# Zero fills in 2 MB pairs of 16 KB rows, and the w_o gradient stored with 2 KB rows

## The chip, the cores and the metric

The kernel runs on one core of a Trainium2 chip. The time is what the device reports for one execution, in microseconds (us). The kernel before took 599.43 us (median of three runs, 598.24 to 599.79). A profile of one execution goes with it; its span runs from the first to the last instruction.

In what follows PE is the engine for matrix products, DVE and ACT are the engines for element-wise work, POOL and SP are the engines that issue most of the DMA transfers here. Each core has 16 DMA engines, and all transfers run on them. POOL's transfers stand in the queue that the profile calls q0, SP's in q1.

## The reference

One token passes through a modulated attention block with a cache and a modulated gated feed-forward block, and then all gradients are computed for the output's gradient `grad_out`.

```python
def _A_ref(x, k_cache, v_cache, wq, wo):      # Hq 32, 4 cache groups, Sk 65536, W 4096
    q = (x @ wq) ...
    k = k_cache[:, :, Sk - W:, :] ...         # the last 4096 positions alone
    v = v_cache[:, :, Sk - W:, :] ...
    p = softmax(q k^T * Dh ** -0.5)
    return (p v) @ wo
mod = silu(c) @ w_mod                         # six parts: sa, ca, ga, sb, cb, gb
h = layernorm(x) * (1 + ca) + sa
x = x + ga * _A_ref(h, A_k_cache, A_v_cache, A_wq, A_wo)
h = layernorm(x) * (1 + cb) + sb
x = x + gb * ((sigmoid(h @ w_gate) * (h @ w_up)) @ w_down)
# outputs: x, and the gradients of A_x, k_cache, v_cache, wq, wo, w_gate, w_up, w_down, c, w_mod
```

The gradients of the two caches have the caches' full shape, 4 groups of 65536 rows of 128 numbers each, and all but the last 4096 rows of each group are zero. So most of what the kernel writes is zeros: 2 x 4 regions of 15 MB.

## The kernel before, in words

**Stages.** In order of time (from the profile): loads of the cache windows and of w_q, the query and the scores (to about 67 us); the N stage, 128 steps of products of keys with weighted values (line 640, to about 155 us); the long product stage, in which 64 chunks (`bch`, line 685) of 8 products each combine w_q and w_o (line 695), mixed with the sections of w_mod (to about 306 us); the feed-forward stage, seven blocks of 512 columns of w_gate and w_up and 512 rows of w_down, forward and backward at once (lines 1022 to 1066, to about 480 us); the end stage, which makes and stores the gradients of w_o (`dwo`, line 1139), w_mod (`sec`, `s2`), the caches' last rows (`dV`, `dK`) and w_q (`dwq_tile`).

**Order.** Nothing is reordered by a scheduler: each engine does its instructions in the order in which the program writes them (`tc.manual_schedule()`), and semaphores hold each back until what it reads or overwrites is ready. POOL issues nearly all transfers, in program order, and SP those of w_down, three small rows, some parts of w_mod, and the last stores.

**Zero fills.** The eight zero regions are seen as 128 rows of 120 KB, one row to a partition. They are cut into 120 units of 1 MB, each 128 rows of 8 KB. `zero(n)` (line 153) issues the next n units on POOL from one tile of zeros, which is held in an 8-bit type and widened to 4 bytes by the transfer. Six of the units, at the places NARROW, leave out the first 8 partitions; what they leave is filled by small transfers apart (lines 160 to 167 and 360). The constants Z_* say how many units go at each place of the program. In the N stage and in the product stage the fills are paced: `zero(Z_N[s], recent(mm, 6))` (line 643) makes the fill wait for a product some steps back, and likewise in `bch` (line 697). Z_SM (line 526) is the number of fills that go as soon as the softmax sum's reciprocal is there, just before the N stage. In the feed-forward stage they go at four places of each block (Z_FFN).

**Loads that the fills stand beside.** w_o is loaded in eight parts of 512 rows (`load_wo`, line 337), w_mod in sections (`b_sec`, line 739; `wm_sec`, line 340). Section 2 has the parts of `ga`; `mod_tiles` (line 344) multiplies its eight tiles into ga_ps, sections 4 and 3 likewise into cb_ps and md_ps, and section 5 into g_ps, from which the feed-forward stage's first operands come. `load_ug` (866) and `store_ug` (870) move the up and gate blocks on POOL, `load_wd` and `store_wd` (854, 857) the w_down blocks on SP.

**The gradient of w_o.** A part u of it is the outer product of the attention output's 512 numbers with a row of 1024, made by DVE in the arena's tile `wo_t[u]` as four pieces of 128 partitions. It is stored so that a partition holds four neighbouring rows of the output, 8 KB in one piece:

```python
def dwo_dram(u):
    return out_5[u * 512:(u + 1) * 512, :].rearrange("(p a) n -> p a n", a=4)
```

For that the 512 numbers have to lie in another order than elsewhere. 16 small products (line 1073) and a copy make `o_perm` from `o_col` between the feed-forward stage and the end stage.

**Tiles.** Most data live in one arena of 192 KB per partition; `vt` (line 104) gives the small tiles beside it.

Of the kernel before, what the change touches and what calls it, by code (L numbers as in the profile page):

```python
# [10 lines left out]
P = 128  # L11
FP32 = mybir.dt.float32
BF16 = mybir.dt.bfloat16
# [11 lines left out]
HQ = 32  # L25
# [26 lines left out]
Z_SM = 4  # L52
Z_N = spread(31, 128)
# [5 lines left out]
def kernel(  # L59
# [43 lines left out]

    def vt(shape, name, dt=FP32):
        return pool.tile(shape, dt, name=name)
# [5 lines left out]
    zeros = vt([P, ZW // 2], "zeros", FP8)  # L111
    rows24 = vt([24, P], "rows24", BF16)
# [7 lines left out]
    ones_f = vt([P, P], "ones_f")  # L120
# [3 lines left out]
    for og in (out_2, out_3):  # L124
        for g in range(G):
            region = og[0, g, 0:SKW, :].rearrange("r d -> (r d)").rearrange("(p x) -> p x", p=P)
            for i in range(region.shape[1] // ZW):
                zregions.append(region[:, i * ZW:(i + 1) * ZW])

    narrow = zregions[0:len(NARROW)]
    wide = zregions[len(NARROW):]
    zleft = []
    while narrow or wide:
        if narrow and (len(zleft) in NARROW or not wide):
            zleft.append((narrow.pop(0), True))
        else:
            zleft.append((wide.pop(0), False))
    nlen = len(NARROW)
    ncount = list(range(1, nlen + 1))  # L140
# [12 lines left out]
    def zero(n, after=None):  # L153
        for _ in range(n):
            if len(zleft) <= keep[0]:
                return
            region, narrow_ = zleft.pop(0)
            first = None
            if narrow_:
                nc.gpsimd.inc_swdge_sem([], [], mode="reset_dge_cursor")  # L160
                n = nlen - ncount.pop()
                first = nc.gpsimd.dma_start(
                    out=rest[0:NS, 0:nlen * 128].rearrange("p (t x) -> p t x", t=2)[:, :, n * 64:(n + 1) * 64],
                    in_=zeros[0:NS, 0:64].rearrange("p (t x) -> p t x", t=1).broadcast_to([NS, 2, 64]))
                ins = nc.gpsimd.dma_start(
                    out=region[8:P, :].bitcast(FP32).rearrange("(t p) x -> p t x", t=2),
                    in_=zeros[0:60, :].rearrange("p (t x) -> p t x", t=1).broadcast_to([60, 2, ZW // 2]))
            else:
                ins = nc.gpsimd.dma_start(out=region.bitcast(FP32), in_=zeros[:, :])  # L169
            if after is not None:  # L170
                dep(first or ins, after)

# [80 lines left out]
    def total_bcast(part, ncol, name, scale):  # L253
        ps = new_acc("tot_" + name)
        nc.tensor.matmul(ps[:, 0:ncol], lhsT=ones_f[:, :], rhs=part[:, 0:ncol], start=True, stop=True)
        tot = vt([P, ncol], name)
        ts(tot, ps[:, 0:ncol], float(scale), ALU.mult)
        return tot

    def layernorm_col(x_col, name, gap=lambda: None):  # L260
# [7 lines left out]
        sq = vt([P, KD], name + "_sq")  # L268
# [13 lines left out]
    def layernorm_bwd_col(dln, ln, rstd, name):  # L282
        part = vt([P, 2], name + "_parts")
        nc.vector.reduce_sum(out=part[:, 0:1], in_=dln, axis=AX.X)
        tmp = vt([P, KD], name + "_tmp")
        ttr(tmp, dln, ln, part[:, 1:2])
        means = total_bcast(part, 2, name + "_means", -1.0 / D)
        dx = vt([P, KD], name + "_dx")
        nc.vector.scalar_tensor_tensor(out=dx, in0=ln, scalar=means[:, 1:2], in1=dln, op0=ALU.mult, op1=ALU.add)
        ts(dx, dx, means[:, 0:1], ALU.add, rstd[:, 0:1], ALU.mult)  # L290
        return dx, means
# [41 lines left out]

    def dwo_dram(u):
        return out_5[u * 512:(u + 1) * 512, :].rearrange("(p a) n -> p a n", a=4)
# [293 lines left out]
    for g in range(G):  # L629
        nbank = bank_pair("n_ps", g)  # L630
        for t_ in range(KT):
# [11 lines left out]
            zero(Z_N[s], recent(mm, 6))  # L643
# [41 lines left out]
    def bch(n=1):  # L685
        for _ in range(n):
# [10 lines left out]
            zero(Z_B[nbq - 1 - len(bq)], recent(mm, 3))  # L697
# [228 lines left out]
    assert not bq  # L926
    fold_half(7, 1)
    zero(Z_FOLD[0])
# [90 lines left out]
    zero(Z_FOLD[2])  # L1019
    load_wd(1, 0)  # L1020
    load_wd(1, 1)
    for q in range(NB):
        z = Z_FFN[q]
        more = q + 1 < NB
        for j in range(KD):
# [12 lines left out]
            if j == 3:  # L1038
                store_ug(q, 0, 4)
                zero(z[0])  # L1040
        store_ug(q, 4, 4)
        zero(z[1])
        if more:
# [13 lines left out]
            zero(z[2])  # L1057
# [3 lines left out]
            zero(z[3])  # L1061
# [3 lines left out]
        else:  # L1065
            zero(z[2] + z[3])
# [3 lines left out]
    op_ps = new_acc("op_ps")  # L1070
    for hh in range(4):
        for a in range(4):
            nc.tensor.matmul(op_ps[32 * hh:32 * hh + 32, 8 * a:8 * a + 8], lhsT=ident_f[:, a::4], rhs=o_col[:, hh::4],
                             start=True, stop=True, tile_position=(0, 32 * hh))
    o_perm = kb_col
    cp(o_perm, op_ps[:, 0:HQ])
# [62 lines left out]
    def dwo(u):  # L1139
        for a in range(4):  # L1140
            outer_dve(wo_t[u][:, a, :], o_perm[:, 8 * a + u:8 * a + u + 1], dattn_b)
        nc.gpsimd.dma_start(out=dwo_dram(u), in_=wo_t[u])
# [134 lines left out]
    x2 = vt([P, KD], "x2")  # L1277
# [4 lines left out]
    dcsum = vt([P, KD], "dcsum")  # L1282
# [3 lines left out]
    t1 = vt([P, KD], "dc_t1")  # L1286
# [4 lines left out]
    dct = vt([P, KD], "dct")  # L1291
    addv(dct, dcs01[:, :, 0], dcsum)
    addv(dct, dct, dcs)
    dcv = vt([P, KD], "dcv")
# [8 lines left out]
    dwq_tile(5)  # L1303
    tail = nc.sync
    s2(2, tail)
# [8 lines left out]
    assert not zleft and not narrow and not jobs and not bq  # L1314
# [29 lines left out]
```

## Time and profile before

| | us |
|---|---|
| median of three runs | 599.43 |
| the profiled execution | 599.43 |
| its span | 597.6 |

| engine | busy us | share of the span |
|---|---|---|
| PE | 410.6 | 69% |
| DVE | 337.4 | 56% |
| ACT | 264.5 | 44% |
| POOL | 155.0 | 26% |

| transfers | count, KB each | us from issue to landing (median) |
|---|---|---|
| zero fills, POOL | 114 x 1024 | 16.7 |
| zero fills, narrow, POOL | 6 x 960 | 12.7 |
| stores of 1 MB, POOL (w_o gradient among them) | 28 x 1024 | 19.2 |
| w_o loads, POOL | 8 x 1024 | 12.6 |
| w_mod loads, POOL | 7 x 1024 | 18.9 |
| w_down loads, SP | 14 x 512 | 10.2 |

How to read the profile: its first rows cut the span into 40 slices of 14.9 us, and a digit is the busy share of a slice in tenths. Below them stand the bytes per second of each slice and the packets of each DMA queue; a packet is what one of the 16 DMA engines moves at a time, and a row of a transfer that is up to 8 KB long is one packet, while rows of 1 or 2 KB go in packets of 4 KB. Lines of a timeline give start, duration, engine, source line and operation; in brackets is the idle time of the engine before, and what ended it. Landings are told by the semaphores that the 16 DMA engines raise.

### The profile page before, as it was taken

What the parts mean: (1) busy time and instruction counts of PE and PEld (TensorE: products, weight loads), DVE (VectorE), ACT (ScalarE), POOL (GpSimd) and SP (SyncE); (2) the same over time, 40 slices, a digit from 0 to 9 for tenths busy, and PEclk for the clock granted to TensorE, in tenths of its full rate; (3) what the DMA queues carried; (4) which work ended last, traced back from release to release, by engine and by line L of the source; (5) the groups of instructions that cost most, each with busy time, mean ns of one, the idle gap of its engine ahead of it and who ended that gap; (6) DMA issues with size and microseconds to landing.
All of it is one profiled execution on the core that took longest, in us unless ns stands there. A gap on an engine that the chain in (4) does not pass through costs nothing. (4 is left out here: it accounts for less than half of the span.)

```text
span 597.6 us, 11102 instructions
## 1 busy us (share of the span) xinstructions
PE 410.6 (69%) x4619; PEld 278.0 (47%) x4644; DVE 337.4 (56%) x642; ACT 264.5 (44%) x408; POOL 155.0 (26%) x254
## 2 busy tenths in 40 slices
PE   3997689999999989899974444544444295785210
PEld 3996434334344446556554433434434265585110
DVE  3654599999511020160019495796786886878350
ACT  3479515558211023212225472754744835793110
POOL 3113213212222222222221342323423252131100
PEclk9999799999999999999985555555555586855555
DMA  8999999999999999999999999999999999999996
GB/s 352 418 418 422 412 425 417 429 424 424 428 421 426 422 428 423 422 424 424 421 401 411 419 404 403 398 390 416 401 399 420 419 422 422 422 423 425 426 423 284
DMA packets 44002, 246.63 MB, mean 413 GB/s; under 512 B 5085, under 2 KB 5085, under 8 KB 22496
## 3 DMA queue, kind: packets, MB, share of 16 engines
q0 software_dynamic: 36656, 218.64, 95.3%
q1 hardware_dynamic: 7248, 27.27, 11.9%
q8 instruction: 36, 0.59, 0.4%
q14 instruction: 14, 0.11, 0.0%
q10 hardware_dynamic: 48, 0.01, 0.0%
HBM read 60.30 MB, written 185.60 MB: 411 GB/s over the span
## 5 line engine op out<-in xcount | busy, mean ns | idle before, releaser
L695 PE MATMUL b_ps<-arena 128*128 128x512 bf16 x494 | 113.4, 379 | 1.0 <-issue 0.2
L169 POOL DMA_DIRECT2D out_dram<-zeros x114 | 62.4, 548 | 173.7 <-DMA out_dram<-zeros 47.4
L840 PE MATMUL tp_side<-ident_bf,arena 128*128 128x128 bf16 x432 | 51.7, 300 | 54.7 <-ACT arena L841 46.0
L193 DVE TENSOR_TENSOR arena<-arena 128x2048 bf16<-128x2048 bf16 x64 | 76.5, 1223 | 2.3 <-PE n_ps L640 0.3
L695 PEld LDWEIGHTS <-arena 128*128 128x128 bf16 x512 | 48.7, 98 | 55.9 <-issue 2.9
L840 PEld LDWEIGHTS <-arena 128*128 128x128 bf16 x432 | 44.3, 141 | 62.3 <-issue 62.1
L841 ACT COPY arena<-tp_side 128x1024 bf16<-128x1024 bf16 x54 | 54.0, 1013 | 40.9 <-PE tp_side L840 40.0
L640 PE MATMUL n_ps<-arena 128*128 128x512 bf16 x249 | 65.1, 378 | 6.9 <-DVE arena L193 5.0
L210 DVE CUSTOM_DVE_ANT_0 arena<-arena,scr 128x1024 bf16<-128x1024 bf16 x56 | 66.2, 1220 | 3.5 <-ACT scr L996 3.5
L210 DVE CUSTOM_DVE_ANT_0 junk<-arena,b1k 128x1024 bf16<-128x1024 bf16 x28 | 34.3, 1223 | 32.8 <-DMA arena<-in_B_w_down_dram 32.2
L640 PEld LDWEIGHTS <-arena 128*128 128x128 bf16 x256 | 24.6, 97 | 41.6 <-issue 16.2
L241 ACT ACTIVATE arena<-scr,h 128x1024 bf16<-128x1024 bf16 x35 | 39.3, 1148 | 0.0
L202 DVE CAST arena<-b_ps 128x512 bf16<-128x512 f32 x6 | 4.2, 692 | 61.6 <-PE b_ps L695 61.6
L1173 ACT ACTIVATE arena<-ps_kv 128x512 bf16<-128x512 f32 x48 | 26.1, 680 | 27.5 <-PE ps_kv L1169 27.4
L1169 PE MATMUL ps_kv<-junk,arena 8*128 8x128 bf16 x256 | 27.4, 305 | 13.7 <-DVE arena L206 12.7
L604 ACT CAST arena<-t_ps 128x512 bf16<-128x512 f32 x56 | 30.1, 589 | 12.1 <-PE t_ps L602 12.1
L872 POOL DMA_DIRECT2D out_dram<-arena x28 | 21.3, 765 | 50.2 <-ACT arena L241 43.5
L1169 PEld LDWEIGHTS <-arena 8*128 8x128 bf16 x256 | 25.2, 141 | 15.6 <-issue 15.5
L996 ACT COPY scr<-tp_dug 128x1024 bf16<-128x1024 bf16 x7 | 7.1, 1012 | 41.5 <-issue 41.5
L459 ACT COPY arena<-tp_wq 128x1024 bf16<-128x1024 bf16 x23 | 21.7, 1041 | 8.1 <-PE tp_wq L457 8.1
L868 POOL DMA_DIRECT2D arena<-in_B_w_up_dram x14 | 10.6, 755 | 49.5 <-DMA out_dram<-arena 29.6
L206 DVE TENSOR_SCALAR arena<-arena,cs_col 128x4096 bf16<-128x4096 bf16 (+1 forms) x16 | 16.1, 1024 | 10.4 <-DMA out_dram<-arena 10.3
(305 smaller groups left out, 640.1 us busy)
## 6 DMA issues: line engine op xcount, KB each, us to landing
out_dram<-zeros POOLq DMA_DIRECT2D x114, 1024.0 KB, 16.7
out_dram<-arena POOLq DMA_DIRECT2D x28, 1024.0 KB, 19.2
out_dram<-arena POOLq DMA_DIRECT2D x30, 512.0 KB, 11.4
out_dram<-arena SPq DMA_DIRECT2D x20, 512.0 KB, 8.6
arena<-in_A_wq_dram POOLq DMA_DIRECT2D x8, 1024.0 KB, 20.8
arena<-in_A_wo_dram POOLq DMA_DIRECT2D x8, 1024.0 KB, 12.6
arena<-in_w_mod_dram POOLq DMA_DIRECT2D x7, 1024.0 KB, 18.9
arena<-in_B_w_down_dram SPq DMA_DIRECT2D x14, 512.0 KB, 10.2
```

What stands on the lines that cost most here:

```text
L169: ins = nc.gpsimd.dma_start(out=region.bitcast(FP32), in_=zeros[:, :])
L193: return nc.vector.tensor_tensor(out=out, in0=a, in1=b, op=op)
L210: return nc.vector.tensor_tensor_reduce(out=out, in0=w, in1=b, scale=1.0, scalar=0.0, op0=ALU.mult, op1=ALU.add, accum_out=acc)
L241: return nc.scalar.activation(out=out, in_=b, func=ACT.Copy, scale=col)
L459: nc.scalar.copy(out=blk, in_=tp[:, :])
L604: nc.scalar.copy(out=o, in_=ps)
L640: mm = nc.tensor.matmul(nbank[k][:, :], lhsT=k_nat[:, g, t_ * DH:(t_ + 1) * DH], rhs=vp[:, t_ % 2, 4 * k:4 * k + 4, :].rearrange("p h d -> ...
L695: mm = nc.tensor.matmul(bbank[p][k][:, :], lhsT=a4[:, p, h, :], rhs=wo_t[u][:, a, k * 512:(k + 1) * 512], start=(i == 0 and a == 0), stop= ...
L840: nc.tensor.transpose(tp[:, i * P:(i + 1) * P], blk[:, i * P:(i + 1) * P], ident_bf[:, :])
L841: nc.scalar.copy(out=blk if dst is None else dst, in_=tp[:, :])
L1169: nc.tensor.matmul(ps[:, t4 * DH:(t4 + 1) * DH], lhsT=rows[32 * g:32 * g + HG, t_ * P:(t_ + 1) * P], rhs=hd[32 * g:32 * g + HG, :], start= ...
L1173: nc.scalar.activation(out=o, in_=ps[:, :], func=ACT.Copy, scale=float(scale))
```

## The change

- `zregions` keeps whole regions. They are cut into pairs (128 rows of 16 KB, 2 MB) and singles (8 KB rows); `zero` takes a pair where two units in a row are due and neither is narrow, unless it is called with `paired=False`, as in the feed-forward stage. 40 of POOL's fills are then pairs, 34 singles, 6 narrow.
- `paced` replaces `zero` in the N stage and the product stage: it keeps account of the units owed and issues an even number at the first that is owed, so every second unit goes earlier than its place.
- Z_SM is 6 instead of 4, and Z_N has 29 units instead of 31.
- The gradient of w_o is stored as it is loaded, each partition holding rows 128 apart, in pieces of 2 KB; `o_perm` and what makes it are gone.
- `dwq_tile(5)` is issued by SP instead of POOL.
- The tile of zeros is twice as long. To make room, small tiles share one tile (`tiny`), `ones_f` is one column, `rows24` lies in the arena, and some late vectors lie in tiles that are free by then.

```diff
-Z_SM = 4
-Z_N = spread(31, 128)
+Z_SM = 6
+Z_N = spread(29, 128)
...
     def vt(shape, name, dt=FP32):
+        words = shape[1] if dt == FP32 else (shape[1] + 1) // 2
+        if dt in (FP32, BF16) and words < 8:
+            k = tiny_n[0]
+            tiny_n[0] += words
+            assert tiny_n[0] <= TINY
+            t = tiny_t[:, k:k + words]
+            return t if dt == FP32 else t.bitcast(BF16)
         return pool.tile(shape, dt, name=name)
...
-    zeros = vt([P, ZW // 2], "zeros", FP8)
-    rows24 = vt([24, P], "rows24", BF16)
+    zeros = vt([P, ZW], "zeros", FP8)
+    rows24 = ar(144, 0.25)[0:24, :]
...
-    ones_f = vt([P, P], "ones_f")
+    ones_f = vt([P, 1], "ones_f")
...
+    for k, region in enumerate(zregions):
+        i = nlen if k == 0 else 0
+        n = region.shape[1] // ZW
+        if (n - i) % 2:
+            singles.append(region[:, i * ZW:(i + 1) * ZW])
+            i += 1
+        pairs.extend(region[:, c * ZW:(c + 2) * ZW] for c in range(i, n, 2))
...
-    def zero(n, after=None):
+    def zero(n, after=None, paired=True):
+        while n > 0 and len(zleft) > keep[0]:
...
+            elif paired and n > 0 and pairs and len(zleft) > keep[0] and not zleft[0]:
+                n -= 1
+                zleft.pop(0)
+                ins = nc.gpsimd.dma_start(out=pairs.pop(0).bitcast(FP32), in_=zeros[:, :])
             else:
-                ins = nc.gpsimd.dma_start(out=region.bitcast(FP32), in_=zeros[:, :])
+                if not singles:
+                    pr = pairs.pop()
+                    singles.extend((pr[:, 0:ZW], pr[:, ZW:2 * ZW]))
+                ins = nc.gpsimd.dma_start(out=singles.pop(0).bitcast(FP32), in_=zeros[:, 0:ZW // 2])
...
+    def paced(n, after):
+        owed[0] += n
+        if owed[0] > 0:
+            k = owed[0] + owed[0] % 2
+            owed[0] -= k
+            zero(k, after)
...
-            zero(Z_N[s], recent(mm, 6))
+            paced(Z_N[s], recent(mm, 6))
...
-            zero(Z_B[nbq - 1 - len(bq)], recent(mm, 3))
+            paced(Z_B[nbq - 1 - len(bq)], recent(mm, 3))
...
-    zero(Z_FOLD[0])
+    zero(Z_FOLD[0] - ahead)
...
-                zero(z[0])
+                zero(z[0], None, False)
...
-    op_ps = new_acc("op_ps")
-    for hh in range(4):
-        for a in range(4):
-            nc.tensor.matmul(op_ps[32 * hh:32 * hh + 32, 8 * a:8 * a + 8], lhsT=ident_f[:, a::4], rhs=o_col[:, hh::4],
-                             start=True, stop=True, tile_position=(0, 32 * hh))
-    o_perm = kb_col
-    cp(o_perm, op_ps[:, 0:HQ])
...
     def dwo(u):
         for a in range(4):
-            outer_dve(wo_t[u][:, a, :], o_perm[:, 8 * a + u:8 * a + u + 1], dattn_b)
-        nc.gpsimd.dma_start(out=dwo_dram(u), in_=wo_t[u])
+            outer_dve(wo_t[u][:, a, :], o_col[:, 4 * u + a:4 * u + a + 1], dattn_b)
+        nc.gpsimd.dma_start(out=wo_dram(out_5, u), in_=wo_t[u])
...
-    dwq_tile(5)
     tail = nc.sync
+    dwq_tile(5, tail)
```

## The prediction

> **What bounds the kernel now.** I read the slices first, then the DMA queues, then the waits and timelines of POOL and PE, and last the packet and landing times that the trace keeps for each transfer.
>
> ```profile
> PE   3997689999999989899974444544444295785210
> DMA  8999999999999999999999999999999999999996
> GB/s 352 418 418 422 412 425 417 429 424 424 428 421 426 422 428 423 422 424 424 421 401 411 419 404 403 398 390 416 401 399 420 419 422 422 422 423 425 426 423 284
> DMA packets 44002, 246.63 MB, mean 413 GB/s; under 512 B 5085, under 2 KB 5085, under 8 KB 22496
> q0 software_dynamic: 36656, 218.64, 95.3%
> q1 hardware_dynamic: 7248, 27.27, 11.9%
> ```
>
> No engine but DMA is full from end to end: bytes over rate is the span. What can move the end is the price of the bytes, or an interval in which the queues have nothing. The waits of POOL, which issues nearly everything, say how the queue is fed:
>
> ```profile
> POOL out_dram L169 <- DMA out_dram<-zeros: 47.4, 26, 3.9
> POOL out_dram L169 <- PE n_ps L640: 42.4, 21, 4.0
> POOL out_dram L169 <- PE b_ps L695: 32.6, 13, 5.3
> ```
>
> The first line is POOL waiting for an older transfer. Its issue times and the landings show why: the k-th POOL transfer always waits for the (k-8)-th, so eight are in flight at most, and from 137 to 315 us there are seven at nearly every issue (they land 14 to 23 us after their issue). POOL's timeline in the long product stage shows one issue per landing:
>
> ```profile
> 192.04 0.77 POOL L341 DMA_DIRECT2D arena<-in_w_mod_dram  x1 [1.44 <-DMA out_dram<-zeros]
> 194.19 0.53 POOL L169 DMA_DIRECT2D out_dram<-zeros  x1 [1.37 <-DMA out_dram<-zeros]
> 196.62 0.53 POOL L169 DMA_DIRECT2D out_dram<-zeros  x1 [1.90 <-DMA out_dram<-zeros]
> ```
>
> PE is nearly full there too, so it has to be asked where PE and DMA meet. PE's timeline has two places:
>
> ```profile
> 210.10 2.04 PE L347 MATMUL ga_ps<-cs_bf,arena 128*128 128x1 bf16 x64
> ...
> 250.45 1.74 PE L347 MATMUL cb_ps<-cs_bf,arena 128*128 128x1 bf16 x64
> ...
> 305.55 0.61 PE L789 MATMUL BT_ps<-ident_bf,scr 128*128 128x128 bf16 x8
> 307.92 1.35 PE L347 MATMUL g_ps<-cs_bf,arena 128*128 128x1 bf16 x48 [1.75 <-DMA arena<-in_w_mod_dram]
> ```
>
> The reader is to see that ga_ps takes 0.30 us more than the equal cb_ps: its second half needs the load issued at 192.04, whose last engine landed at 211.14, about when PE gets there. And before the feed-forward stage PE waits 1.75 us for a load.
>
> **Part 1, the fills (zero, paced).** Of 120 MB-units, 80 go as 40 pairs, 34 stay single (27 of them from the feed-forward stage's first fills on), 6 stay narrow. The pair's packet size is nowhere on POOL's queue; I build its price. On one engine the commonest packet of 2 KB takes 84 ns, of 4 KB 159 ns, of 8 KB 309 ns: 9 ns each plus 36.6 ns per KB. The 64 KB that one engine has of a 1 MB fill are 2400 ns by the slope alone. Landing to landing, a fill after a fill takes 2448 ns (mean over the 16 engines, median of 83). So 48 ns per fill belong to packets and to the completion, and a pair, with as many packets and one completion for twice the bytes, can save at most 48: 40 x 48 = 1.9 us. The slow engines lose more: within one fill's landing the first-to-last spread grows from 1.95 us (52.58 to 54.53) to 3.48 us (254.35 to 257.83). They need about (3.48-1.95)/86 = 18 ns more per transfer. If half or all of that is paid per packet, pairs save up to 40 x 66 = 2.6 us. The low bound is nothing saved, and below it a loss, if 16 KB rows are cut: that is a rival below. I take 1.9, since the rows that make it are this same operation, and 2.6 as one end.
>
> POOL's issues fall by 40 x 0.55 us (L169's mean); they run inside the 173.7 us in which POOL waits before them, so they count nothing.
>
> **Part 2, order and pacing.** Each fill's place in q0 decides when the loads behind it land. Counting MB-units in both orders ahead of each load: w_o part 0 has 2 more, part 4 has 3 more, parts 5 to 7, the second w_mod load (b_sec(2,4), 192.04), both of section 4 and the first of section 3 one more; the others, the feed-forward loads too, are equal. One more is 2.45 us later. Only b_sec(2,4) has no slack: with 23 pairs ahead of it (1.1 us saved) it lands 1.35 us later, about 212.5, and PE, at its tiles near 211.1, stalls about 1.4 us. The others have 4.8 us (245.61 against 250.45) or more. Six fills instead of four after rsum: at that issue (67.63) two transfers are still in flight until 71.83, so q0 is covered before and after; nothing.
>
> With pairs, eight in flight are up to 16 MB, so POOL runs with PE and not with the landings. In one queue that changes no order, so I cost it at nothing; the cover is q0's backlog.
>
> **Part 3, SP's loads behind fat packets.** The loads of w_down and two of w_mod on q1 (SP, issued 284.07 to 300.28) were first served at 295.45, 11.4 us after their issue, and from 295.5 to 299.5 had 157 GB/s beside q0's 249. If rows of 16 KB halve q1's turns and double its wait, q1 starts when q0's fills before the feed-forward loads are through: those would take 300.5 us, less 1.9, so about 299 to 301 with PE's 1.4. Then 1 MB at half of the 400 GB/s that 4 KB packets move (5.2 us) and 0.5 MB of 2 KB packets at about 125 (its rate at 304 to 306; 4.2 us) end near 310.4 instead of 308.25. So g_ps and the feed-forward stage start 1 to 3 us later. Does that reach the end? At that stage's last stores (472.72) q0's backlog runs to 478.57, 5.85 us. Fills that are done 1.9 us sooner leave 3.95. A start 2 us later stays under it: nothing.
>
> [...]
>
> **Part 4, w_o's gradient (dwo).** Eight stores of 1 MB go from 8 KB rows to 2 KB rows. Store after store with 8 KB rows: 2453 ns. With 1 KB rows (w_up/w_gate gradients, beside no other queue): 1276 for half, 2552 per MB. Loads with 2 KB rows (w_o after w_o): 2625. Those show as 4 KB packets. Packets alone (2 x 159 against 309) give 9 x 1024 / 16 = 0.6 us in all, the low bound: no shorter row was cheaper in any stage. The ends by rows are 8 x 0.10 = 0.8 and 8 x 0.17 = 1.4; I take 1.1, between the same direction and the same row length. POOL's issue grows from 0.53 to 0.77 us, under 7 in flight.
>
> [...]
>
> The permutation goes: 32 matmuls on PE at 466.6 to 468.1, in PE's slack, and a copy of 0.18 us on the chain at 476.08. DMA has 2 us or more of backlog there: nothing, at most -0.2.
>
> **Part 5, tail and small edits.** dwq_tile(5) goes from POOL to SP. [...] Behind it q0 and q1 still hold work to 591, so the same bytes end at the same time; 0, bounds +-0.5. The packed small tiles, one column of ones, and the memset of zeros (twice as long, under 4.75 us of POOL's wait for vecs): 0.
>
> **Sum.** The profiled execution is 599.43 (span 597.6 and 1.8 around it), also the median of the three. -1.9 + 1.1 = -0.8: **598.6 us**.
>
> **Rivals.** (1) Slow engines gain too. For: their spread collapses in the feed-forward stage (389.09 to 390.94, one at 392.31), so the others wait for them. -2.6 + 0.6 - 0.2, and up to half of that 3.5 us spread: 595.5 to 597.2. (2) The feed-forward stage starts late past its backlog. Place: g_ps; it decides from 3.95 us of delay, and is slower than before from 4.75. If q1's first turn comes 5.5 us late, with PE's 1.4 that is 6.9, and 598.6 + 2.95 = 601.5. Against it: q0's packets turn to 4 KB at about 300 anyway. (3) The row of 16 KB is cut into 4 KB packets, the change does not do what it says: 16 x 159 + 9 = 2553 against 2448 is +0.105 per MB, 80 MB are +8.4, with dwo 608.9. Against: 8 KB rows were not cut, and the instruction queue shows 16 KB packets (at 1010 ns median, 62 ns per KB, dearer than 36.6; that queue feeds no output, so it sets no price here).
>
> **How the numbers follow.** The forecast (597.8 to 600.5) has 0.45, rival 1 0.30, rival 2 0.15, rival 3 0.07, others 0.03. About 0.3% (1.8 us) is what a measurement of this kernel can tell from no change. Faster by that takes rival 1 and little else: 0.31. Within: the forecast and a third of rival 2: 0.47. Slower: 0.22. The range leaves out rival 3 and the ends of 1 and 2: 596.2 to 601.6.
>
> **What would show it.** On the page: about 5100 packets fewer on q0 from fills, 1024 more from dwo. Landing intervals of pairs of 4.85 us or less (right), 4.90 (nothing saved), 5.1 (cut). ga_ps longer by about 1.4 us; g_ps starting after 308.5. dwo's landings 2.55 to 2.63 us apart. The slices of the product stage at 426 to 432 GB/s. What would make it wrong: slices below 9 at 300 to 480 us, or a tail whose last engine is later by more than a microsecond.

## The result, and the profile after

The changed kernel takes 605.01 us (median of 20 executions, 600.81 to 607.84); the kernel before takes 599.41 us (20 executions beside it). The ratio is 1.0079, with a 95% interval of 1.0055 to 1.0103: the change costs 0.8%. I had forecast 598.6 us, and 0.22 for slower. Here and below a ratio leaves out executions more than 1.5% above their kernel's fastest (three of e1's twelve, six of e4's, two of e12's, one of e13's), which the medians keep, so a median can show a larger loss than its ratio. The executions of the changed kernel spread with PE's clock: the nine with the longest times, 606.62 us and above, have a mean granted clock of 0.767 or less, the eleven others, 605.55 and below, 0.768 or more. Which of the two makes the other is not told by this: PE's clock is 0.50 in the feed-forward stage (from 309.98 to 484.06 us in the profile of before, from 316.28 to 490.36 in that of the changed kernel), so a stage that lasts longer lowers the mean too. The profiled one took 607.84 (span 606.1), so its rows show the loss at its largest: 8.4 us more than the profile of before.

The page of the changed kernel, the rows that answer to those shown of before:

```profile
PE   3998679999999989999874454444445196684220
PEclk9998899999999979989995555555555576955555
DMA  8999999999999999999999599999999999999997
GB/s 352 418 418 425 413 429 426 431 428 424 430 426 421 431 429 419 435 419 428 408 412 360 197 404 418 381 397 411 404 405 407 416 420 416 421 419 426 425 423 304
DMA packets 39266, 246.63 MB, mean 407 GB/s; under 512 B 4445, under 2 KB 4445, under 8 KB 23904
q0 software_dynamic: 31776, 217.59, 91.2%
q1 hardware_dynamic: 7392, 28.32, 12.4%
```

PEclk is the clock that PE was granted, in tenths of full speed. The same row of before:

```profile
PEclk9999799999999999999985555555555586855555
```

The reader sees three things. The fills did become cheaper: of the 4th to the 19th slice, eleven are at 425 GB/s or more, where before had five. Nearly all the loss is in one place, the 22nd and 23rd slice (318 to 349 us), with 360 and 197 GB/s. And PEclk has two slices below 9 in the product stage, the 15th and the 18th, where before has 9 until the slice in which that stage ends (the 21st).

Six microseconds at a time, the hole looks like this (stretch; busy time of PE, PEld, DVE, ACT, POOL; granted clock, DMA share, GB/s):

```profile
328.00:334.00 6.00, 2.58 (x46) 2.37 (x47) 5.15 (x14) 1.16 (x3) 0.00 (x0) 0.50 0.79 292
334.00:340.00 6.00, 2.48 (x21) 2.00 (x19) 6.00 (x12) 4.40 (x5) 0.00 (x0) 0.50 0.81 272
340.00:346.00 6.00, 3.03 (x24) 2.54 (x24) 5.86 (x12) 5.85 (x7) 1.94 (x3) 0.50 0.15 55
```

POOL has issued the last fill ahead of the stage by 317.8, and its next instruction is the first store of the feed-forward stage. POOL's timeline, after and then before:

```profile
316.19 1.64 POOL L185 DMA_DIRECT2D out_dram<-zeros  x3
344.06 1.52 POOL L896 DMA_DIRECT2D out_dram<-arena  x2 [26.23 <-ACT arena L266]
```

```profile
320.70 0.53 POOL L169 DMA_DIRECT2D out_dram<-zeros  x1 [1.85 <-DMA out_dram<-zeros]
331.05 1.52 POOL L872 DMA_DIRECT2D out_dram<-arena  x2 [9.82 <-ACT arena L241]
```

Before, three of POOL's transfers were still in flight at that store, and the last fill landed at 339.37, 8.3 us after it. After, the store comes 13.0 us later, the last fill has landed at 334.13, and POOL's queue is empty for 9.9 us.

Why is the stage late? PE's waits between 60 and 330 us, and its timeline at g_ps, the stage's first input:

```profile
PE g_ps L371 <- DMA arena<-in_w_mod_dram: 6.2, 2, 4.4
...
PE md_ps L371 <- issue: 2.2, 1, 2.2
...
PE b_ps L719 <- DMA arena<-in_A_wo_dram: 0.9, 1, 0.9
...
PE ga_ps L371 <- DMA arena<-in_w_mod_dram: 0.8, 1, 0.8
```

```profile
313.98 0.94 PE L371 MATMUL g_ps<-tiny,arena 128*128 128x1 bf16 x32
316.64 0.37 PE L371 MATMUL g_ps<-tiny,arena 128*128 128x1 bf16 x8 [1.71 <-DMA arena<-in_w_mod_dram]
321.46 0.38 PE L371 MATMUL g_ps<-tiny,arena 128*128 128x1 bf16 x8 [4.45 <-DMA arena<-in_w_mod_dram]
```

PE is done with the product stage at 314.15 instead of 306.16, 8.0 us late. Then it waits for the two w_mod tiles that SP loads, wm_sec(5,4) and wm_sec(5,5). SP can issue those only when PE is done with what lies in their place (line 945 of the changed kernel), so they are late with PE. SP's waits between 280 and 325 us say so:

```profile
SPq L365 <- PE b_ps L719: 13.3, 2, 7.4
```

The load wm_sec(5,5) is issued at 308.27 instead of 300.28. It also takes longer, 13.1 us instead of 8.0, and lands at 321.41 instead of 308.25: 13.2 us late, of which 8.0 are PE's and 5.2 its own.

PE's 8.0 us are waits of 0.92 (w_o), 0.77 (ga_ps) and 2.16 us (md_ps), and time at half clock. PE's timeline behind ga_ps, a microsecond of the same stretch, and the same seven products in before:

```profile
210.96 0.94 PE L371 MATMUL ga_ps<-tiny,arena 128*128 128x1 bf16 x32
212.67 0.95 PE L371 MATMUL ga_ps<-tiny,arena 128*128 128x1 bf16 x32 [0.77 <-DMA arena<-in_w_mod_dram]
213.70 3.01 PE L719 MATMUL b_ps<-arena 128*128 128x512 bf16 x7
```

```profile
214.00:215.00 1.00, 1.00 (x4) 0.40 (x3) 0.36 (x3) 0.00 (x0) 0.00 (x0) 0.50 0.94 377
```

```profile
212.21 1.67 PE L695 MATMUL b_ps<-arena 128*128 128x512 bf16 x7
```

Seven products that took 1.67 us in before take 3.01, at a granted clock of 0.50. There are three such stretches between 160 and 310 us, at 213.9, 224.1 and 258.25, each 3.41 us long; before has none. At a clock of 0.50 each can cost PE at most half of its length, 1.7 us.

So the story of this one profile has four links: a load lands later; PE waits and then runs at half clock for a while; SP's last load is issued late and lands later still; POOL's queue runs dry before the stage has anything to store. The experiments take the links one by one.

### The profile page after: what moved, and what is told of

It reads as the page before. It is cut to its first block, busy times and chain, and to the rows that moved or that the text cites. A ratio compares the mean times of both kernels' runs of the same rounds, so it can differ in the third digit from the quotient of the medians.

```text
span 606.1 us, 10967 instructions
## 1 busy us (share of the span) xinstructions
PE 414.2 (68%) x4587; PEld 279.2 (46%) x4612; DVE 338.7 (56%) x641; ACT 264.8 (44%) x408; POOL 138.0 (23%) x213
## 5 line engine op out<-in xcount | busy, mean ns | idle before, releaser
L719 PE MATMUL b_ps<-arena 128*128 128x512 bf16 x494 | 117.8, 389 | 2.1 <-DMA arena<-in_A_wo_dram 0.9
L719 PEld LDWEIGHTS <-arena 128*128 128x128 bf16 x512 | 50.0, 100 | 59.8 <-issue 9.4
L864 PEld LDWEIGHTS <-arena 128*128 128x128 bf16 x432 | 44.8, 142 | 62.3 <-issue 62.1
L180 POOL DMA_DIRECT2D out_dram<-zeros x40 | 21.7, 543 | 134.3 <-PE b_ps L719 52.8
L664 PEld LDWEIGHTS <-arena 128*128 128x128 bf16 x256 | 24.6, 97 | 41.6 <-issue 16.2
L185 POOL DMA_DIRECT2D out_dram<-zeros x34 | 19.3, 570 | 32.1 <-PE q_ps L499 14.3
## 6 DMA issues: line engine op xcount, KB each, us to landing
out_dram<-zeros POOLq DMA_DIRECT2D x34, 1024.0 KB, 13.2
out_dram<-arena POOLq DMA_DIRECT2D x30, 512.0 KB, 10.9
```

The costliest lines, as they stand in the source:

```text
L180: ins = nc.gpsimd.dma_start(out=pairs.pop(0).bitcast(FP32), in_=zeros[:, :])
L664: mm = nc.tensor.matmul(nbank[k][:, :], lhsT=k_nat[:, g, t_ * DH:(t_ + 1) * DH], rhs=vp[:, t_ % 2, 4 * k:4 * k + 4, :].rearrange("p h d -> ...
L719: mm = nc.tensor.matmul(bbank[p][k][:, :], lhsT=a4[:, p, h, :], rhs=wo_t[u][:, a, k * 512:(k + 1) * 512], start=(i == 0 and a == 0), stop= ...
L864: nc.tensor.transpose(tp[:, i * P:(i + 1) * P], blk[:, i * P:(i + 1) * P], ident_bf[:, :])
```

## The experiments

I started with two theories. **Theory A**: the rows of 16 KB, or the 16 MB that pairs put in flight, hold up SP's loads and PE's instruction fetches. **Theory B**: the order is to blame; `paced` issues each pair when its first unit is owed, so one more MB stands ahead of some loads.

This table has the profiled execution of every run; the median and the ratio to the kernel before follow below, run by run. "Load" is the last load that g_ps needs, wm_sec(5,5); "in flight" counts POOL's transfers at the stage's first store; the rate is that of 310 to 345 us. One execution need not be like the median: e3's is the slowest of its twelve, those of e1, e4, e9, e11 and e16 are the fastest or second fastest of theirs.

| kernel | load issued, landed | first store | in flight | GB/s | profiled us |
|---|---|---|---|---|---|
| before | 300.28, 308.25 | 331.05 | 3 | 416 | 599.43 |
| after | 308.27, 321.41 | 344.06 | 0 | 309 | 607.84 |
| e1 8 KB halves | 303.75, 313.33 | 335.91 | 1 | 389 | 602.26 |
| e2 lagging pairs | 301.93, 309.49 | 331.46 | 3 | 414 | 599.04 |
| e3 2 KB rows alone | 304.71, 316.37 | 339.01 | 0 | 376 | 601.97 |
| e4 late fills single | 303.50, 315.03 | 337.67 | 0 | 366 | 603.38 |
| e5 one fill ahead | 311.35, 322.61 | 345.25 | 0 | 330 | 608.45 |
| e6 one pair held | 300.90, 312.20 | 334.85 | 1 | 380 | 602.11 |
| e7 idle products | 307.11, 321.42 | 344.07 | 0 | 315 | 606.81 |
| e8 lag, work in waits | 298.72, 308.81 | 331.43 | 3 | 415 | 598.93 |
| e9 own tile | at 5.85 | 333.00 | 2 | 408 | 599.03 |
| e10 busy 2.4 us | 305.93, 317.41 | 340.06 | 0 | 371 | 603.78 |
| e11 busy 4.8 us | 306.54, 319.58 | 342.23 | 0 | 346 | 604.86 |
| e12 lag, Z_SM 8 | 302.35, 317.03 | 339.68 | 0 | 352 | 603.91 |
| e13 one ahead, busy | 306.03, 317.63 | 340.27 | 0 | 360 | 604.86 |
| e14 lag, own tile | at 5.9 | 333.81 | 2 | 413 | 599.72 |
| e15 e14 and work | at 5.9 | 331.37 | 3 | 416 | 599.75 |
| e16 e14, 2 MB pairs | at 5.8 | 330.96 | 3 | 416 | 597.08 |

Wherever the load is issued by PE's pace, the first store follows its landing by 22.0 to 22.8 us. That is the last two links in one row: when the load is late the store is late, and where at most one transfer is in flight by then, the rate is 389 GB/s or less and the time 601.97 us or more; with two or three it is 408 or more. e3's row shows that the loss can come without any change of the order: its median is 599.31, and this execution, with PE waiting 0.71 us at ga_ps and the load landing at 316.37, took 601.97. The kernel before has executions as slow (up to 603.39), none of them profiled. With the change they are the rule: its fastest of 20 took 600.81. With 35 us at 309 instead of 416 GB/s, after loses 9.0 us there.

### Rows or order: e1, e2, e4

e1 keeps the changed order and drops the rows of 16 KB:

```diff
-                ins = nc.gpsimd.dma_start(out=pairs.pop(0).bitcast(FP32), in_=zeros[:, :])
+                pr = pairs.pop(0)
+                first = nc.gpsimd.dma_start(out=pr[:, 0:ZW].bitcast(FP32), in_=zeros[:, 0:ZW // 2])
+                ins = nc.gpsimd.dma_start(out=pr[:, ZW:2 * ZW].bitcast(FP32), in_=zeros[:, 0:ZW // 2])
```

> The changed kernel with every pair issued as two transfers of 1 MB and 8 KB rows, at the same place, in the same order, with the same wait. Theory A (the rows of 16 KB themselves, or the 16 MB they put in flight, keep SP's loads and PE's instruction fetches waiting, and so the feed-forward stage starts 13 us late): the loss goes; the last SP load before g_ps lands near 308 to 311, POOL's queue stays full at 330 to 345, and the time is that of the kernel before plus 0.5 (w_o gradient): 599.5 to 600.5. Theory B (the order: one MB more ahead of the loads, PE waits at w_o and ga_ps, and the half-clock stretches follow): nothing or little is won, 604 to 606, and ga_ps still waits.

Measured: 607.18 us, ratio 1.0074 (1.0039 to 1.0108). Theory A falls as the cause of the loss: without a single row of 16 KB the loss is about the same (1.0079 for the changed kernel). The sign that I had named for theory B is not in the profile, though: this execution took 602.26, PE came to ga_ps at 212.47, later than in the changed kernel (210.96), and did not wait there.

e2 keeps the pairs and changes when they go:

```diff
-        if owed[0] > 0:
-            k = owed[0] + owed[0] % 2
+        if owed[0] > 1:
+            k = owed[0] - owed[0] % 2
```

> The changed kernel with paced() issuing a pair when two units are owed instead of when the first is, so that no load has more ahead of it than in the kernel before from the product stage on. Theory A: the waits of PE on w_o and ga_ps go, but the loads of SP are as slow as in the changed kernel (about 13 us for wm_sec(5,5)) and PE's wait in md_ps stays: 602 to 605. Theory B: 598 to 599.5, since the pairs' 1.7 us are then won.

Measured: 599.22 us, ratio 1.0002 (0.9980 to 1.0025). This is what theory B said: 40 pairs of 16 KB rows, and the loss is gone (one of the twelve executions still took 605.90). PE's timeline of e2 at ga_ps and g_ps shows no wait at the first and a short one at the second:

```profile
212.06 1.74 PE L371 MATMUL ga_ps<-tiny,arena 128*128 128x1 bf16 x64
...
309.53 0.35 PE L371 MATMUL g_ps<-tiny,arena 128*128 128x1 bf16 x8 [0.74 <-DMA arena<-in_w_mod_dram]
```

The gain that theory B promised as well is hardly there (0.33 us below the median of before, within the interval). In e2's profile the queue is short of work at 94 to 98 us (317 and 346 GB/s) and the feed-forward stage has some slices lower than before's (the 26th 379 against 398).

e4 makes the last seven pairs before the stage single again:

```diff
-            paced(Z_B[nbq - 1 - len(bq)], recent(mm, 3))
+            paced(Z_B[nbq - 1 - len(bq)], recent(mm, 3), nbq - 1 - len(bq) < 40)
...
-    zero(Z_FOLD[0] - ahead)
+    zero(Z_FOLD[0] - ahead, None, False)
```

(the third argument of `paced` goes to `zero` as `paired`).

> The changed kernel with the last seven pairs before the feed-forward stage (from about 265 us on) as singles, so that SP's loads and ug loads stand beside 8 KB rows; 33 pairs stay. Theory A in the form that SP's loads alone matter: wm_sec(5,5) takes 8 us again instead of 13, PE's earlier waits stay, the stage starts 6 to 8 us late instead of 13, and the time falls to 601 to 602.5. Theory B: PE's early waits are what counts, 604 to 605.

Measured: 607.41 us, ratio 1.0069 (1.0035 to 1.0103). SP's last load takes 11.5 us beside rows of 8 KB too, against 13.1 in the changed kernel. Rows of 16 KB beside SP's loads at the end are not needed for the loss.

### One fill: e5, e6

e5 is the kernel before with one number of its pacing moved by one chunk:

```diff
-Z_B = [n + (i in (31, 38)) for i, n in enumerate(spread(29, 43))] + ...
+Z_B = [n + (i in (31, 38)) + (i == 15) - (i == 16) for i, n in enumerate(spread(29, 43))] + ...
```

> The kernel before with one thing changed: one zero fill of 1 MB, paced by the chunk after it, goes on POOL ahead of the second w_mod load of section 2 (b_sec(2,4)) instead of behind it. Theory B (order: ga_ps waits for that load, PE stalls and runs at half clock for some microseconds after, the loads that SP issues behind PE come late, POOL's queue runs dry at 330 to 345): the whole loss from this one fill, 602 to 607, ga_ps with a wait of 1 to 2.5 us. Theory D (it takes several loads one MB later, the w_o parts above all): 599.5 to 600.5.

Measured: 608.05 us, ratio 1.0109 (1.0063 to 1.0155). One fill of 1 MB on the other side of one load costs 8.8 us at the median, 6.5 by the ratio; no pair, no other change is needed. (Two of the six executions took 601.25 and 602.61, the others 607.82 and more.) PE's timeline of e5:

```profile
210.13 0.94 PE L347 MATMUL ga_ps<-cs_bf,arena 128*128 128x1 bf16 x32
213.42 0.97 PE L347 MATMUL ga_ps<-cs_bf,arena 128*128 128x1 bf16 x32 [2.35 <-DMA arena<-in_w_mod_dram]
...
317.07 1.14 PE L347 MATMUL g_ps<-cs_bf,arena 128*128 128x1 bf16 x40
322.66 0.37 PE L347 MATMUL g_ps<-cs_bf,arena 128*128 128x1 bf16 x8 [4.45 <-DMA arena<-in_w_mod_dram]
```

With a wait of 2.35 us at ga_ps PE is 10.9 us late at g_ps (317.07; in before it was ready at 306.16).

e6 is the opposite: the changed kernel with the one pair behind that load.

```diff
-        if owed[0] > 0:
+        if owed[0] > 0 and not hold:
...
-            paced(Z_B[nbq - 1 - len(bq)], recent(mm, 3))
+            paced(Z_B[nbq - 1 - len(bq)], recent(mm, 3), nbq - 1 - len(bq) in (14, 15))
```

(`hold` is a new third argument of `paced`.)

> The changed kernel with one pair moved: the one that paced() issues at chunk 14, ahead of b_sec(2,4), is held until that load has been issued. All else, the w_o parts with one MB more ahead of them too, is as in the changed kernel. Theory B: 598.5 to 600, no wait in ga_ps. Theory D: 602 to 605, and PE still waits for w_o.

Measured: 601.63 us, ratio 1.0033 (1.0009 to 1.0058), between what the two theories gave. More than half of the loss goes with this one pair, not all. The rest shows at g_ps:

```profile
306.62 1.14 PE L371 MATMUL g_ps<-tiny,arena 128*128 128x1 bf16 x40
312.25 0.37 PE L371 MATMUL g_ps<-tiny,arena 128*128 128x1 bf16 x8 [4.49 <-DMA arena<-in_w_mod_dram]
```

PE is on time here (306.62), and the load was issued at 300.90, only 0.6 us after that of before, yet it takes 11.3 us instead of 8.0. By the trace's packets, q1 moves 64 to 180 GB/s while q0 has the 4 KB packets of the ug(0) loads (297 to 307 us in e6) and 23 GB/s from 307, when q0 is back at fills. The load's last data packet (2 KB, a row of one partition: the 256 KB loads of w_mod on q1 go in packets of 2 KB, 512 in before, not of 4 KB) ends at 308.06, only 0.6 us later than in before (307.50), so what is missing are completions, as I call the 4-byte packets (16 for each of SP's four loads here in before): four of them began between 307.2 and 308.6 and took 2.5 to 4.3 us, the last until 311.69. In e2 q1 has 109 GB/s until 308, the data end at 308.79, the last completion at 308.80, and the load lands at 309.49. So in these two runs it counted whether the load fitted, completions and all, into a stretch that q0 set. Here rows of 16 KB have a share after all: where q0 moves 8 KB rows, no completion of q1 between 280 and 330 us took more than 2.2 us in any run, beside 16 KB rows up to 3.7 (after), 4.3 (e6, e12). That pairs bring q0 back to its fills sooner is how I read e6 against e2; no run tried it alone.

### Idle or busy: e10, e11, e13, e7

Does a late PE cost so much, or an idle PE? e10 is the kernel before with PE made late by work, its transfers untouched:

```diff
+    busy = new_ps("busy")
+    nrot[0] -= 1
+    for _ in range(11):
+        nc.tensor.matmul(busy[:, :], lhsT=ident_bf[:, :], rhs=wo_t[0][:, 0, 0:512], start=True, stop=True)
     ga_ps = new_acc("ga_ps")
```

> The kernel before, its order of transfers untouched, with 11 products of 128x512 that nothing reads ahead of ga_ps: PE is busy for about 2.4 us more instead of idle for 2.4 us as in e5. If the idle time with the half-clock stretches behind it is what costs (e5 had five such stretches, 8 us of PE), this costs what 2.1 us of lateness cost: 599.5 to 602, and shows no half-clock stretch. If any 2.4 us of lateness are enough: 605 to 608 as e5.

Measured: 604.12 us, ratio 1.0057 (1.0028 to 1.0086). So 2.4 us of lateness without idle time cost 4.5 us at the median, 3.4 by the ratio, more than I expected of work without idle time and less than in e5. In its profile, which has one half-clock stretch where I had expected none, PE comes to this place 2.2 us later than in before (212.30; over all the runs this varies from 209.5 to 213.0), the load is issued 5.7 us later than in before and then takes 11.5 us. The slack that my prediction relied on is not there.

e11 has 22 products instead of 11:

```diff
-    for _ in range(11):
+    for _ in range(22):
```

> As e10 with 22 products, 4.8 us. It gives the price of PE's lateness without idle time. By the prediction's slack (3.95 us and more of backlog) 599.5 to 601.5; if SP's last load is caught by the fills and made later by 3 to 5 us more, 602 to 605.

Measured: 608.79 us, ratio 1.0128 (1.0080 to 1.0177), more than expected: another 2.4 us cost about as much again as the first (4.7 at the medians, 4.3 by the ratios).

e13 is e5 with e10's products: the load is as late as in e5, but PE is busy while it comes.

> The kernel of e5 (one fill ahead of b_sec(2,4), 608.05 us) with the 11 unread products of e10 ahead of ga_ps: the load is as late as in e5, but PE waits busy instead of idle. If the 4 us by which e5 is slower than e10 come from the half-clock stretches that follow idle time, this is e10: 603 to 605, few such stretches. If they come from the order itself, it stays at 607 to 609.

Measured: 603.37 us, ratio 1.0054 (1.0025 to 1.0083), that of e10, and 4.7 us below e5 at the median, 3.3 by the ratio. PE's timeline of e13:

```profile
212.43 2.54 PE L760 MATMUL busy<-arena,ident_bf 128*128 128x512 bf16 x11
214.81 1.74 PE L347 MATMUL ga_ps<-cs_bf,arena 128*128 128x1 bf16 x64
...
311.75 1.14 PE L347 MATMUL g_ps<-cs_bf,arena 128*128 128x1 bf16 x40
```

PE leaves ga_ps 2.2 us later than in e5 (216.55 against 214.39) and is at g_ps 5.3 us sooner (311.75 against 317.07). In e5 the clock is 0.50 in five stretches of 3.41 us between 160 and 310 us (two of them adjacent), in e13 in one. How much that is shows in PE's time from the end of ga_ps to the end of the product stage, the same work in every kernel listed (e7, e8 and e15 do other work there):

| half-clock stretches in it | PE's time, us |
|---|---|
| 0 (before, e2, e6) | 94.0, 94.0, 94.0 |
| 1 (e1, e4, e9, e10, e11, e13) | 95.4 to 95.7 |
| 2 (e12, e14, e16) | 96.8 to 97.1 |
| 3 (e3) | 98.5 |
| 3, and a wait of 2.16 (after) | 100.5 |
| 5, and a wait of 1.32 (e5) | 102.8 |

Each stretch costs 1.3 to 1.7 us. So products that nothing reads, in place of idle time, go with 4.7 us less at the median. The two intervals overlap a little; of the executions, four of e5's six took 607.82 us or more, one of e13's twelve. The two profiles are not quite alike either: in e13 PE came to this place 2.3 us later than in e5, so its wait would have been shorter without the products too. Stretches come without a late load as well (two in e14), behind PE's regular waits of 2.15, 0.80 and 0.73 us. What the late load adds, as far as these profiles show, is more idle time, and more stretches.

e7 tried the same on the changed kernel with short products in the waits for DVE and ACT (`idle(n)` issues n products of 128x64):

```diff
+    idle(24)
     bcast(ln2_bf, KD, ln2_b, "AA")
...
-    bcast(cf_bf, KD, cf_b, "AA")
+    idle(8)
+    bcast(cf_bf, KD, cf_b, "AA", lambda: idle(8))
```

> The changed kernel with products added that nothing reads: 24 of 128x64 before the broadcast of ln2, 8 and 8 before the two halves of the broadcast of cf, in the stretches where PE waits for DVE or ACT (2.15, 0.80 and 0.73 us). They do no work and can only cost PE time. If the half-clock stretches are what turns small waits into 8 us of lateness (theory B's second link), the ones at 224 and 258 go, 3.4 us of PE time come back, and the time falls to 600 to 604. If only the waits themselves count, it stays at 605 to 607.

Measured: 606.76 us, ratio 1.0116 (1.0091 to 1.0140): nothing won. The products were too short to fill the waits (0.86 us of 2.15), and the profile has a new wait of 2.94 us in the middle of them that no semaphore explains. The run tells the theories apart in neither direction; e13 does.

### The load that waits for PE: e9, e14

e9 is e1 (8 KB rows, changed order, 607.18) with wm_sec(5,5) in a tile of its own, which the half-length tile of zeros leaves room for:

```diff
+    g5 = vt([P, 1024], "g5", BF16)
...
+    g_t[5] = g5
...
+    nc.sync.dma_start(out=g5, in_=wm_view[:, 5, 5 * D:6 * D])
     load_wd(0, 0)
...
-    wm_sec(5, 5, 1, 60, nc.sync)
```

> The kernel of e1 (the changed order in 8 KB rows, 607.18 us) with one load moved: the last w_mod tile that g_ps needs, wm_sec(5,5), gets a tile of its own and is issued by SP ahead of load_wd(0,0), some 15 us sooner, so that no load of SP but wm_sec(5,4) has to wait for PE's last chunks. PE is as late as in e1. If PE's lateness is made larger by that load (it is issued when PE gets there, misses the stretch in which POOL's queue runs the ug loads, and waits until the fills behind them are through), the time falls to 600 to 603. If PE's lateness alone is what costs, it stays at 605 to 607.

Measured: 601.43 us, ratio 1.0021 (0.9992 to 1.0051): 5.7 us below e1 at the median, 3.2 by the ratio. Nine of e1's twelve executions lie above the slowest of e9 (603.78). Since nothing holds the load back now, SP issued it at 5.85 us and not at 285, as I had meant. PE's timeline of e9:

```profile
212.27 0.94 PE L374 MATMUL ga_ps<-tiny,arena 128*128 128x1 bf16 x32
214.12 0.95 PE L374 MATMUL ga_ps<-tiny,arena 128*128 128x1 bf16 x32 [0.91 <-DMA arena<-in_w_mod_dram]
...
310.59 1.14 PE L374 MATMUL g_ps<-tiny,arena 128*128 128x1 bf16 x40
311.59 0.34 PE L374 MATMUL g_ps<-tiny,g 128*128 128x1 bf16 x8
```

PE still waits, 3.21 us for w_o (at 177.33) and 0.91 at ga_ps, and is still 4.4 us late at g_ps (310.59), but the last tile is there, and this execution, one of the two fastest, takes 599.03. PE's lateness by itself costs 1.9 us at these medians, not clear of nothing by the interval; through the load that it holds back it costs the rest.

e14 has both remedies, e2's two lines and e9's tile; as in e9, its fills are all in 8 KB rows. The tile together with 16 KB rows was not tried.

> Lagging pacing (e2) and the tile of its own for wm_sec(5,5) (e9) together, fills in 8 KB rows: no load later than in the kernel before and no SP load behind PE's last chunk. If these two links are the whole cause, nothing of the loss is left: 598.2 to 599.3, with hardly an execution above 601.

Measured: 599.32 us, ratio 1.0005 (0.9992 to 1.0017). Nothing of the loss is left, and eleven of twelve executions lie below 601 us (the other at 601.07). Its profile has two half-clock stretches (255 to 262) and PE at g_ps at 311.34, 5 us late, and still takes 599.72.

### The rest: e3, e8, e12, e15, e16

e3 is the kernel before with the w_o gradient alone in 2 KB rows; the products of `op_ps` are gone:

```diff
-            outer_dve(wo_t[u][:, a, :], o_perm[:, 8 * a + u:8 * a + u + 1], dattn_b)
-        nc.gpsimd.dma_start(out=dwo_dram(u), in_=wo_t[u])
+            outer_dve(wo_t[u][:, a, :], o_col[:, 4 * u + a:4 * u + a + 1], dattn_b)
+        nc.gpsimd.dma_start(out=wo_dram(out_5, u), in_=wo_t[u])
```

> The kernel before with the w_o gradient alone stored in 2 KB rows and o_perm gone. Both theories: the prediction's step said +1.1 us (600.5); the landing intervals of the changed kernel say +0.5 (599.9). Ratio 1.000 to 1.002.

Measured: 599.31 us, ratio 0.9994 (0.9980 to 1.0009): between -1.2 and +0.5 us.

e8 is e2 with three chunks of products moved into PE's waits (`bcast` calls its last argument between its two halves); e15 is e14 with the same:

```diff
+    bch(1)
     bcast(ln2_bf, KD, ln2_b, "AA")
...
-    bcast(cf_bf, KD, cf_b, "AA")
+    bch(1)
+    bcast(cf_bf, KD, cf_b, "AA", bch)
...
-    bch(5)
+    bch(3)
     b_sec(3, 4, 40)
```

> The changed kernel with pacing that lags (as in the run of that kind) and with three chunks of the product stage moved into the same three waits of PE, so that they are filled with work that has to be done anyway. PE should end the product stage about 3 us sooner (303 instead of 306), wm_sec(5,5) land near 305, and the time be 597 to 599, below both kernels, if the feed-forward stage's start still bounds anything; 599 if it doesn't.

> e14 with the three chunks moved into PE's waits (e8). With wm_sec(5,5) out of the way the feed-forward stage can start as early as PE and wm_sec(5,4) let it: 597.5 to 599 if an earlier start is worth anything, else as e14.

Measured: 599.29 us, ratio 1.0000 (0.9981 to 1.0019), and 599.79 us, ratio 1.0007 (0.9990 to 1.0023). An earlier PE wins nothing, and the load did not land near 305 as I had expected: in e8 SP's load is issued 3.2 us sooner than in e2 and lands 0.7 us sooner; that it waits for the ug loads' stretch is how I read this.

e12 is e2 with eight units right behind the softmax sum:

```diff
-Z_SM = 6
-Z_N = spread(29, 128)
+Z_SM = 8
+Z_N = spread(27, 128)
```

> A version meant to beat both: the lagging pairs of e2 (599.22) with eight units instead of six right behind the softmax sum and 27 paced in the N stage, since e2's queue was short of work at 94 to 98 us (317 and 346 GB/s there). That loss is 0.7 us: 598.3 to 599.0, at most 0.2% under the kernel before.

Measured: 603.39 us, ratio 1.0038 (1.0007 to 1.0069), wrong: not faster but slower. The load was issued 0.4 us later than in e2 (302.35) and landed 7.5 us later; its data were through 3.7 us later (312.52 against 308.79), and 4-byte completions beside 16 KB rows, up to 4.3 us long, made the rest. Two half-clock stretches (220 and 254) stand ahead of it in this profile. Whether they come from the order or from the execution, one profile can't tell.

e16 is e14 with each pair again one transfer, reading the 2 KB tile twice:

```diff
+                ins = nc.gpsimd.dma_start(
+                    out=pairs.pop(0).bitcast(FP32).rearrange("p (t x) -> p t x", t=2),
+                    in_=zeros[:, :].rearrange("p (t x) -> p t x", t=1).broadcast_to([P, 2, ZW // 2]))
```

> e14 with each pair again one transfer of 2 MB, its zeros read twice from the 2 KB tile, so that one completion serves 2 MB. If the pieces are 8 KB packets, the completion alone is saved, up to 40 x 0.04 us: 597 to 598.5. If the source's 2 KB cut the packets smaller, 600 or more.

Measured: 598.69 us, ratio 0.9985 (0.9966 to 1.0004). The packets are of 8 KB (19792 on q0, none of 16 KB). It is the fastest of all, 1% below the changed kernel; against the kernel before the interval just reaches 1, so a gain of 0.15% is possible and not shown. If there is one, the completions do not make it: two pairs in a row land 4.892 us apart (median of 26), no nearer than two single fills did in before (4.896). Its page has no hole:

```profile
DMA  8999999999999999999999899999999999999997
```

## Why the prediction was wrong

**Part 1, right in size.** Pairs land 4.854 us apart (median) where two single fills took 4.896: 0.042 each, 1.7 us for 40, against 1.9. (In e2 it is 4.865, 1.2 us for 40.) The 16 KB rows went as 5120 packets of 16 KB, 649 ns each (median); rival 3 is out. I had put the 48 ns down to packets and completion together; e16, with one completion to a pair but 8 KB packets, saves nothing (4.892), so the saving goes with the number of packets. The slope that I wrote as 36.6 ns per KB is 37.5 by the three packet times, and the 2400 ns use 37.5.

**Part 2 is the step that failed.** For b_sec(2,4) its counting was right to a tenth: it was to land at about 212.5 and landed at 212.62. Three things beside it were wrong. First, "the others have 4.8 us or more": w_o part 3, which I had counted as unchanged, has 43 units ahead of it instead of 42, landed 1.6 us later, at 175.97, and PE waited 0.92 for it; I had not checked its slack. Second, I priced PE's stall at its own length, 1.4 us. The stall was shorter (0.77), but PE ran at half clock for 3.41 us right after it, and with two more such stretches and a wait in md_ps it was 8.0 us late. Third, "in one queue that changes no order, so I cost it at nothing" holds for q0, not for q1, whose loads go when PE lets SP issue them.

**Part 3, right in kind, wrong in size.** Without PE's lateness (e2) the load landed at 309.49 and the stage's start cost nothing, as worked out (310.4, nothing). That rows of 16 KB halve q1's turns and double its wait was an assumption of mine; no run shows turns, and q1's first packet came 0.5 us later than in before. And I let the load be late by a fixed 1 to 3 us. It was issued by PE's pace and served in a stretch that q0 set, and where it missed that stretch it landed 4 to 14 us later than in before.

**The slack, wrong.** I took 3.95 us from the backlog at the end of the feed-forward stage. The place that decides is its start: three transfers in flight, and 8.3 us until the last fill has landed. With PE done 5.7 us late in e10, the first store was 9.0 us late: these 8.3 us are soon used up.

**Part 4, too dear.** 2.516 us per MB against 2.453 is 0.5 us in all, not 1.1; e3 can't tell it from nothing. The permutation, the other small edits and the move of dwq_tile(5) were not tried alone.

**Rival 2 was right in its outcome**, the feed-forward stage starting late past its backlog, with 0.15. It named the place (g_ps), and its bound (slower from 4.75 us of delay) isn't far off: e6, late by 3.95 us in its profile, cost 2.4 us, e2 with 1.24 nothing. What it gave as the reason did not happen: q1's first packet came at 295.99, 0.5 us later than in before (295.45) and not 5.5. The delay came from PE (8.0 us) and from the last load itself (5.2). Its price was too low, 601.5, because the delay was put at 6.9 us; it was 13.2 in the profile.

## What to carry to other kernels

Before a transfer is moved in a queue, list every load behind it with the microseconds between its landing and its use; where that is under one transfer's time, the move can cost more than that transfer takes (2.45 us for the fill of e5, 8.8 us of loss at the median). Price a stall by what the stalled engine releases, not by its length: here PE's lateness went into a load that SP could issue only behind PE, and from there into an empty queue. A load that gates a stage belongs in a place that is free early; 2 KB per partition took back 5.7 us at the median.

## What the hardware showed that I had not expected

**The clock fell after short stalls.** The three half-clock stretches of the changed kernel start at 213.88, 224.12 and 258.25 and last 3.41 us each; they lie 3.00 and 10.0 such lengths apart, so they keep to a fixed grid. The clock records of both traces agree: between the first and the last, every stretch at full or at half clock lasts a whole number of times 3.413 us, from 2 to 71 in before and from 1 to 51 in the changed kernel. In the 3.41 us ahead of the three stretches PE was not idle throughout: it had 0.77, 2.14 and 0.80 us without a product. Another such length with 0.92 us, at w_o, brought none, nor did the 3.21 us at w_o in e9, which the grid divides into 1.15 and 2.06. The first and the third also held 1.7 to 1.9 us of products with a single column; whether these play a part was not tried. How much idle time brings such a stretch on stays open.

**q1 got nearly nothing beside fills.** From 285 to 295 us in before, with loads issued from 284.07 on, q1 moved no packet while q0 moved 8 KB rows at 427 GB/s; in the changed kernel it moved 2 to 20 GB/s from 309 to 314, beside 16 KB rows, and q0 414. Some 4-byte completions of q1's transfers took 1.3 to 3.7 us there, where 9 ns is the median. Most come in steps, of 0.30 us where q0 moves 8 KB rows (0.66, 0.96, 1.27 and so on to 2.18) and of 0.60 us beside 16 KB rows (to 4.29); the longest is about seven steps long in either case. What a step is, and why q1 got so little, is open.

**A wait that no semaphore explains.** In md_ps PE stopped for 2.16 us (1.32 in e5; in e7 it was 2.94, among the added products), and each time went on 1.45 to 1.56 us after a packet of the instruction queue had been read (294.04 to 295.10 in the changed kernel). PE may have been out of instructions; no run tried it.
